# Two score chunks at a time, PSUM releases ranked first, and an output tile cut in three, in a fused attention and GELU kernel

## The chip, the cores and the metric

The kernel runs on one core of one Trainium2 chip. A core has five engines with instruction streams of their own: TensorE (matrix products, PE in the profile), VectorE (DVE), ScalarE (ACT), GpSimd (POOL) and SyncE (SP, which here only starts transfers). TensorE writes to PSUM, a small memory of eight banks, from which VectorE and ScalarE bring results back to the main on-chip memory. Transfers to and from device memory run on 16 DMA engines, fed by queues of SP, ScalarE and GpSimd.

The metric is the device time of one execution in microseconds (us), the median over several runs.

## What is computed

```python
# q, k, v: 8 batches x 12 heads x 448 x 64, float32
q_n = q / (norm(q) + 1e-06)
k_n = k / (norm(k) + 1e-06)
scores = q_n @ k_n.T / tau                  # tau = 0.1
attn = exp(scores - max); attn /= sum(attn)
x = (attn @ v)                              # heads side by side: 3584 x 768
h = x @ w_in                                # 768 x 2048
g = h * sigmoid(1.702 * h)
out = g @ w_out                             # 2048 x 768, float32
```

Each query's 448 scores lie within 1/tau of zero, so the kernel subtracts no maximum that depends on the data.

## The kernel before

**Work items.** Two heads of a batch make a pair `x`; there are 48, six to a batch. A pair is loaded (`load`), squared on ScalarE (`square`), summed and turned into inverse norms on VectorE, scaled to fp16 on GpSimd (`scale`; the queries of pair 0 on VectorE), and transposed, for pairs 0 to 11 on TensorE and VectorE, later by a DMA on SP's queue. From pair 12 on (batches 2 to 7) a pair's scores come in four chunks of 112 keys. One chunk (`scores`, L383 to L392) is two matmuls of 448 columns, one for each head, each using 64 of TensorE's 128 rows, into one `sp` tile of two PSUM banks; there are two such tiles. ScalarE takes the exponential of a chunk (`exp`, L397). Two attention products per pair follow (`attend`, L412: 16 matmuls into one bank `a`), each normalised by VectorE (`normalise`, L423 and L426, called `nx`), which frees the bank; then a DMA transposes the result (`turn`, L436). Pairs 0 to 11 do the same in halves of the queries (`scores_h`, `attend_h`, `normalise_h`, `turn_h`, `turned_h`), with the attention in one of the three `mm` banks, which the copy `turned_h` (called `x`) frees.

**The second part.** For each batch 16 products with `w_in` (`mm1`, L511: six matmuls of 448 columns) are followed by a tanh on ScalarE (`tanh`, L521) and a gate on VectorE (`gate`, L528), which frees the product's `mm` bank. The products with `w_out` (`mm2`, L566) run over output tiles of 128 tokens `t`, 28 in all, in two column halves `n` of `NW` = 384; a half is 16 matmuls, planned in four parts. ScalarE scales each half by 0.5 into `ost` (`halve`, L577), and `store` (L591 to L597) writes a tile in one or two runs of rows (`segments`). Only the last tile is stored half by half.

**What sets the order.** Nothing of the order is left to a scheduler in the compiler. `Plan` holds every operation with its engine, an assumed duration, a due time, what must precede it (`after`), and what buffers it takes and frees. `Plan.order` plays all engines forward in time: an engine that is idle starts, of its ready operations whose buffers are free, the one with the smallest due time. An operation on TensorE that changes between 64-row and 128-row matmuls is given `SWITCH_US` more. The order found is what each engine's stream is built in; at run time every engine works strictly through its stream. In the first 50 us of the plan, gaps on TensorE are filled with idle transposes (`fill`, L357).

Due times: a pair's scores, attention and `nx`/`x` are due at `s` to `s + 3`, with `s` two per pair (one per pair in batch 0); reductions 8 (4) before; the tail operations of products, that is tanh, gate and `ost`, `URGENT` = 12 before their product:

```python
add(("s", x, c), "PE", 0.19, s + c // 2, partial(scores, x, c), after=[("qkT", x)],
    takes=[("sp", 1)], frees=[("qkT", int(c == C - 1))], rows=64)
...
add(("nx", x, j), "DVE", 0.55, s + 2 + j, partial(normalise, x, j), after=[("at", x, j)],
    takes=[("xf", 1 - j)], frees=[("a", 1)])
```

Of the kernel before, what the change touches and what calls it, by code (L numbers as in the profile page):

```python
# [10 lines left out]
FP32 = mybir.dt.float32  # L11
# [7 lines left out]
RS_A, RS_B = 0.703952253, 0.703952253 * 2.38924456  # L19

SEM_US = 0.1
SWITCH_US = 0.12
DMA_US = 1.9
LATE_FROM, LATE_US, URGENT = 80.0, 2.0, 12
DMA_ENGINES, DMA_PKT_US, DMA_KB_US = 16, 0.024, 0.037
# [129 lines left out]
def kernel(  # L155
# [23 lines left out]
    AHEAD = 3  # L179
    SQP, SQT, XA, CA, TA, POW = (), (0, 1), (), (0, 1), (), range(HP, 2 * HP)  # L180
    TURN = 2 * HP
    SH = S // 2
    inv_tau = float(1.0 / tau)
    shift = max(0.0, inv_tau - 10.0)
# [195 lines left out]
    def queries(x, j, s0, s1):  # L380
        return qkTs[x][64 * j : 64 * (j + 1), 1, s0:s1]

    def scores(x, c):  # L383
        sp = sps[x, c] = ps_s.tile([128, 2, 512], FP32, name="sp")
        for j in range(2):
            nc.tensor.matmul(  # L386
                out=sp[:, j, :S],
                lhsT=keys(x, j, c),
                rhs=queries(x, j, 0, S),
                start=True,  # L390
                stop=True,
            )  # L392

    def exp(*key):
        e = exps[key] = ets[len(exps) % NE]
# [153 lines left out]
    def gate_h(h, m):  # L549
# [9 lines left out]
            op1=ALU.mult,  # L559
        )  # L560

    def mm2(b2, t, n, part):
        if part == 0:
            mms[b2, t, n] = ps_m.tile([128, 512], FP32, name="mm")
        for kk in range(4 * part, 4 * part + 4):
            nc.tensor.matmul(  # L566
                out=mms[b2, t, n][:, :NW],
                lhsT=gts[b2][:, kk, 128 * t : 128 * (t + 1)],
                rhs=w_out_sb[:, kk, NW * n : NW * (n + 1)],
                start=(kk == 0),  # L570
                stop=(kk == KT2 - 1),
            )

    def halve(b2, t, n):
        if n == 0:
            osts[b2, t] = p_o.tile([128, DM], FP32, name="ost")
        nc.scalar.activation(  # L577
            out=osts[b2, t][:, NW * n : NW * (n + 1)],
            in_=mms.pop((b2, t, n))[:, :NW],
            func=AF.Copy,  # L580
            scale=0.5,
        )
# [5 lines left out]
            yield i0, n  # L588
            i0 += n

    def store(b2, t, i0, n, cols):  # L591
        b, c, p0 = 2 * b2 + i0 // S, (i0 % S) // P, i0 % P
        rows = out[b * S : (b + 1) * S].rearrange("(p c) m -> c p m", c=C)[c]
        nc.sync.dma_start(
            out=rows[p0 : p0 + n, cols],
            in_=osts[b2, t][i0 - 128 * t : i0 - 128 * t + n, cols],
        )  # L597
# [31 lines left out]
    for x in range(NPAIR):  # L629
# [3 lines left out]
        for ti, nm in ((1, "k"), (0, "q")):  # L633
            add(("load", nm, x), "ACT" if x + ti == 0 else "SP", 0.5, s - 13, partial(load, x, (q32, k32)[ti], (q, k)[ti], nm + "32"),
                takes=[(nm, 1)], dma=PAIR, hold=hold, turn=True)
            pl = sq_pool(x, ti)
            add(("sq", ti, x), "POOL" if pl else "ACT", 1.0 if pl else 0.53, early + ti * 0.1, partial(square, x, ti),
                after=[("load", nm, x)], takes=[("sq", 1), ("port", int(pl))], frees=[("port", int(pl))])
            add(("red", ti, x), "DVE", 0.6, early + 0.2, partial(reduce, x, ti),
                after=[("sq", ti, x)], frees=[("sq", 1)])  # L640
            dve = x == 0 and ti == 0
            add(("scale", ti, x), "DVE" if dve else "POOL", 0.7 if dve else 1.0, early + 0.5 if first else s - 5 - ti * 0.1,
                partial(scale, x, ti, nc.vector if dve else nc.gpsimd),
                after=[("norm", 1, grp)], takes=[("qks", 1), ("port", 1)], frees=[(nm, 1), ("port", 1)])
# [25 lines left out]
        if x < HALF:  # L670
            for h in range(2):
                sh = x + HP * h if first else s + h
                for u in range(2):
                    key = (x, h, u)
                    add(("s",) + key, "PE", 0.2, sh, partial(scores_h, *key), after=[("qkT", x)] + [("s", min(x + AHEAD, HP - 1), 0, 1)] * (first and h),
                        takes=[("sp", 1)], frees=[("qkT", h * u)], rows=64)
                    add(("exp",) + key, "ACT", 0.82, sh + 0.1, partial(exp, *key), after=[("s",) + key],
                        takes=[("exp", 1)], frees=[("sp", 1)])
                es = [("exp", x, h, u) for u in range(2)] + [("cast", x)]
                add(("at", x, h), "PE", 0.48, sh + 1, partial(attend_h, x, h), after=es,  # L680
                    takes=[("mm", 1)], frees=[("exp", 2), ("vt", h)])
                add(("nx", x, h), "DVE", 0.65, sh + 1, partial(normalise_h, x, h), after=[("at", x, h)],
                    takes=[("xs", 1)])
                add(("turn", x, h), "PE", 0.15, sh + 1, partial(turn_h, x, h), after=[("nx", x, h)],
                    frees=[("xs", 1)])
                add(("x", x, h), "ACT" if x in XA and not h else "DVE", 0.35, sh + 1, partial(turned_h, x, h), after=[("turn", x, h)],
                    takes=[("x", 1 - h)], frees=[("mm", 1)])
            continue
        for c in range(C):
            add(("s", x, c), "PE", 0.19, s + c // 2, partial(scores, x, c), after=[("qkT", x)],  # L690
                takes=[("sp", 1)], frees=[("qkT", int(c == C - 1))], rows=64)
            add(("exp", x, c), "ACT", 0.82, s + c // 2 + 0.1, partial(exp, x, c),
                after=[("s", x, c)], takes=[("exp", 1)], frees=[("sp", 1)])
        for j in range(2):
            es = [("exp", x, c) for c in range(C)] + [("cast", x)]
            if j == 1:
                es.append(("nx", x, 0))
            add(("at", x, j), "PE", 0.475, s + 2 + j, partial(attend, x, j), after=es,
                takes=[("a", 1)], frees=[("exp", 4 * j), ("vt", j)])
            add(("nx", x, j), "DVE", 0.55, s + 2 + j, partial(normalise, x, j), after=[("at", x, j)],  # L700
                takes=[("xf", 1 - j)], frees=[("a", 1)])
        add(("x", x), "SP", 1.0, s + 4, partial(turn, x), after=[("nx", x, 1)],
            takes=[("x", 1)], frees=[("xf", 1)], dma=packets(256, 512))
# [11 lines left out]
    for b in range(B):  # L715
# [18 lines left out]
                  [("g", int(b % 2 == 0 and u == units[0]))], [("th", 1), ("mm", 1)])])  # L734
        tiles = (0, 1, 2) if b % 2 == 0 else (3, 4, 5, 6)
        for t in tiles:
            for n in range(2):
                for part in range(4):
                    if b:
                        after = [("g", b, 4 * part + 3)]  # L740
                    else:
                        after = [("g", h, 4 * part + 2, "h") for h in range(1 + (t > 0))]
                    after.append(("w_out", part // 2))
                    after += [("mm2", b2, t, n, part - 1)] if part else []
                    last = t == tiles[-1] and n == 1 and part == 3
                    tail = []
                    if part == 3:
                        tail = [("ost", "ACT", 0.4, partial(halve, b2, t, n), [("ost", 1 - n)], [("mm", 1)])]
                        split = b == B - 1 and t == tiles[-1]
                        if n == 1 or split:  # L750
                            cols = slice(NW * n, NW * (n + 1)) if split else slice(0, DM)
                            segs = list(segments(b2, t))
                            for i, (i0, rows) in enumerate(segs):
                                tail.append((("st", i), "SP", packets(rows, 4 * (cols.stop - cols.start)),
                                    partial(store, b2, t, i0, rows, cols), [],
                                    [("ost", int(n == 1 and i == len(segs) - 1))]))
                    product(("mm2", b2, t, n, part), 0.652, partial(mm2, b2, t, n, part), after,
                        [("mm", int(part == 0))], [("g", int(last and b % 2))], tail)

    total, done = sum(u[1] for u in moe), 0.0  # L760
    for name, us, emit, after, takes, frees, tail in moe:
        b, part = divmod(B * done / total, 1)
        start, end = moe_due(b), moe_due(b + 1)
        due = start + (end - start) * part
        done += us
        add(name, "PE", us, due, emit, after=after, takes=takes, frees=frees)
        prev = name
        for kind, eng, n, e, tk, fr in tail:
            if eng == "SP":
                add(kind + name[1:], eng, 0.5, due, e, after=[prev], frees=fr, dma=n)  # L770
            else:
                me = (kind,) + name[1:]
                before = [prev]
                if kind == "ost":
                    me = me[:-1]
                    if me[-1]:
                        before.append(me[:-1] + (0,))
                add(me, eng, n, due - URGENT, e, after=before, takes=tk, frees=fr)
                prev = me
    for i in range(2):  # L780
# [55 lines left out]
```

## Time and profile before

| | |
|---|---|
| median of 13 runs | 439.76 us (438.3 to 440.81) |
| the profiled execution's own time | 439.13 us |
| its span, first to last instruction | 437.3 us |
| TensorE busy | 424.9 us (97%), 4161 matmuls |
| VectorE busy | 237.4 us (54%) |
| ScalarE busy | 306.9 us (70%) |
| GpSimd busy | 151.3 us (35%) |
| granted TensorE clock | 0.998 of full speed |
| exponentials L397 | 192, mean 920 ns |
| products L511, L566 | 672 of 448 columns, 896 of 384 columns |

The span is what the profiler saw from the first to the last instruction; the execution's time is 1.8 us longer. In the tables below a line number such as L386 is that of the kernel before. Busy times of matmuls count each from its start to its modelled end, and since matmuls overlap, the cost of one is the distance to the start of the next.

### The profile page before, as it was taken

The numbers are of one execution on the slowest core, as the hardware profiler recorded it, in microseconds if no ns is written. First come the engines' busy times: TensorE is split into PE (matmuls) and PEld (weight loads), VectorE is DVE, ScalarE is ACT, GpSimd is POOL, SyncE is SP. The second block draws the span as 40 slices with busy tenths as digits, with TensorE's granted clock in tenths as the row PEclk, the third lists the DMA queues.
The fourth block names the chain that finished last, engine by engine and source line by source line (L and its number), as shares of the span: only waits on it lengthen the run. The fifth ranks groups of instructions, "written<-read, shape, count | busy, mean of one in ns | idle before, by whom it ended". The sixth has DMA issues, their size and how long they took to land.

```text
span 437.3 us, 10541 instructions
## 1 busy us (share of the span) xinstructions
PE 424.9 (97%) x4161; PEld 260.1 (59%) x4161; DVE 237.4 (54%) x612; ACT 306.9 (70%) x490; POOL 151.3 (35%) x203
## 2 busy tenths in 40 slices
PE   8899999999999998999999999999999999999996
PEld 8668777555555654565555655565555655565563
DVE  4767978885886759653775338641542125404400
ACT  5899977859999868767896678766776566314411
POOL 2843997375527564242060604242100000000000
PEclk9999999999999999999999999999999999999999
DMA  8999397999997999477555676565112130021022
GB/s 233 250 229 254 76 209 186 274 252 286 211 211 157 257 221 228 116 162 180 155 132 153 175 182 135 142 116 136 35 26 48 49 97 14 12 73 36 2 72 72
DMA packets 95888, 63.99 MB, mean 146 GB/s; under 512 B 56288, under 2 KB 90848, under 8 KB 95840
## 3 DMA queue, kind: packets, MB, share of 16 engines
q1 hardware_dynamic: 91952, 56.81, 55.3%
q0 software_dynamic: 3648, 6.29, 8.0%
q8 instruction: 32, 0.52, 0.5%
q10 hardware_dynamic: 240, 0.23, 0.2%
q14 instruction: 16, 0.13, 0.1%
HBM read 45.61 MB, written 11.01 MB: 129 GB/s over the span
## 4 chain that ended last, share of the span: by engine, by line
PE 60%; DMA 2%; POOL 1%; DVE 1%; SPq 0%; ACT 0%; issue 0%; DVEq 0%; ACTq 0%
PE mm L566 26%; PE mm L511 24%; PE avp L412 6%; PE sp L386 5%; POOL qks L325 1%; DMA k<-in_k_dram 1%; DMA qkT<-qks 1%; DVE gT L528 0%; DVE n L251 0%; SPq L232 0%; SPq L366 0%; ACT sq L245 0%; ACT ost L577 0%; DVE t L291 0%; DVE t L280 0%
## 5 line engine op out<-in xcount | busy, mean ns | idle before, releaser
L397 ACT ACTIVATE et<-sp 112x896 f16<-112x896 f32 x192 | 167.4, 920 | 37.2 <-PE sp L386 32.4
L566 PE MATMUL mm<-w_out,gT 128*128 128x384 f16 x896 | 154.7, 326 | 0.6 <-ACT ost L577 0.6
L511 PE MATMUL mm<-xT,w_in 128*128 128x448 f16 x672 | 135.4, 353 | 1.4 <-DVE gT L528 1.4
L566 PEld LDWEIGHTS <-gT 128*128 128x128 f16 x896 | 83.8, 98 | 66.0 <-issue 14.2
L511 PEld LDWEIGHTS <-w_in 128*128 128x128 f16 x672 | 62.4, 98 | 69.0 <-issue 15.6
L528 DVE SCALAR_TENSOR_TENSOR gT<-th,mm 128x448 f16<-128x448 f16 x112 | 68.7, 616 | 61.0 <-ACT th L521 61.0
L521 ACT ACTIVATE th<-mm 128x448 f16<-128x448 f32 x128 | 69.9, 549 | 33.4 <-PE mm L511 30.5
L251 DVE TENSOR_REDUCE n<-sq 112x8 f32<-112x512 f32 x96 | 63.2, 677 | 28.0 <-ACT sq L245 27.7
L341 POOL CAST vt<-v 112x256 f16<-112x256 f32 x92 | 35.0, 404 | 118.6 <-PE avp L412 70.9
L577 ACT ACTIVATE ost<-mm 128x384 f32<-128x384 f32 x56 | 27.7, 495 | 44.9 <-PE mm L566 43.3
L412 PEld LDWEIGHTS <-et 112*128 112x128 f16 x1152 | 44.6, 97 | 11.4 <-issue 0.2
L325 POOL TENSOR_TENSOR qks<-k,y 112x512 f16<-112x512 f32 x36 | 37.6, 1045 | 31.4 <-DVE y L292 23.2
L423 DVE RECIPROCAL rcx<-avp 128x4 f32<-128x4 f32 x72 | 12.9, 180 | 63.0 <-PE avp L412 62.4
L412 PE MATMUL avp<-vt,et 112*128 112x65 f16 x1152 | 46.7, 193 | 0.0
L386 PE MATMUL sp<-qkT 64*128 64x448 f16 x288 | 40.9, 355 | 0.0
L325 POOL TENSOR_TENSOR qks<-q,y 112x512 f16<-112x512 f32 x36 | 37.6, 1045 | 0.0
L245 ACT ACTIVATE sq<-k 112x512 f32<-112x512 f32 x48 | 30.4, 637 | 6.5 <-DMA k<-in_k_dram 5.2
L426 DVE TENSOR_TENSOR xf<-avp,rcx 128x256 f16<-128x256 f32 x72 | 30.5, 424 | 2.5
L245 ACT ACTIVATE sq<-q 112x512 f32<-112x512 f32 x48 | 30.4, 638 | 1.6 <-DVE n L251 1.4
L541 PE MATMUL mm<-xT,w_in 128*128 128x224 f16 x192 | 21.0, 259 | 0.9 <-DVE gT L553 0.9
L308 POOL TENSOR_TENSOR n<-n,root_of 112x16 f32<-112x16 f32 x6 | 17.4, 2904 | 11.7 <-DVE n L251 11.7
L357 PE MATMUL tps<-ident 128*128 128x128 f16 x241 | 18.1, 234 | 3.2 <-DVE qkT L361 1.8
(44 smaller groups left out, 229.6 us busy)
## 6 DMA issues: line engine op xcount, KB each, us to landing
k<-in_k_dram SPq DMA_DIRECT2D x48, 224.0 KB, 4.4
v<-in_v_dram SPq DMA_DIRECT2D x48, 224.0 KB, 4.8
q<-in_q_dram SPq DMA_DIRECT2D x47, 224.0 KB, 4.7
w_in<-in_moe_w_in_dram POOLq DMA_DIRECT2D x2, 1536.0 KB, 16.2
w_out<-in_moe_w_out_dram POOLq DMA_DIRECT2D x2, 1536.0 KB, 14.4
out_dram<-ost SPq DMA_DIRECT2D x7, 336.0 KB, 3.2
out_dram<-ost SPq DMA_DIRECT2D x8, 288.0 KB, 2.8
out_dram<-ost SPq DMA_DIRECT2D x8, 240.0 KB, 3.0
```

Source lines behind the costliest of these rows:

```text
L245: return nc.scalar.activation(out=sqs[x, ti], in_=src, func=AF.Square)
L251: nc.vector.tensor_reduce(out=n2s[grp][:, x - grp[0], ti], in_=sqs.pop((x, ti)), axis=AX.X, op=ALU.add,)
L325: return eng.tensor_tensor(out=qkss[x][:, 1 - ti].rearrange("p c j d -> p j c d"), in0=src, in1=rss[x][:, ti, :, :, None].to_broadcast((P, ...
L341: copy(out=vt[:, :, j, :D], in_=src[:, j]) for j in range(2)
L386: nc.tensor.matmul(out=sp[:, j, :S], lhsT=keys(x, j, c), rhs=queries(x, j, 0, S), start=True, stop=True,)
L397: nc.scalar.activation(out=e[:, : 2 * S].rearrange("p (j s) -> p j s", j=2), in_=sps.pop(key)[:P, :, :S], func=AF.Exp, scale=inv_tau, **kw,)
L412: nc.tensor.matmul(out=ps[:, (D + 1) * t : (D + 1) * (t + 1)], lhsT=exps[x, c][:, q0 : q0 + 128], rhs=values(x, c, D * j, D * j + D + 1), ...
L426: nc.vector.tensor_tensor(out=xfs[x][:, :, j], in0=ps[:, :, j : j + D], in1=r[:, :, None].to_broadcast((128, 4, D)), op=ALU.mult,)
L511: nc.tensor.matmul(out=ps[:, :S], lhsT=w_in_sb[:, kk, 128 * m : 128 * (m + 1)], rhs=xTs[b, kk][:, :S], start=(kk == 0), stop=(kk == KT1 - 1),)
L521: nc.scalar.activation(out=ths[key], in_=mms[key][:, :S], func=AF.Tanh, scale=0.851)
L528: nc.vector.scalar_tensor_tensor(out=gts[b // 2][:, m, (b % 2) * S : (b % 2 + 1) * S], in0=ths.pop((b, m)), scalar=1.0, in1=mms.pop((b, m) ...
L566: nc.tensor.matmul(out=mms[b2, t, n][:, :NW], lhsT=gts[b2][:, kk, 128 * t : 128 * (t + 1)], rhs=w_out_sb[:, kk, NW * n : NW * (n + 1)], st ...
```

## The change

1. The plan's entry for scores now stands for two chunks: `scores(x, c0)` issues chunks `c0` and `c0 + 1`, four matmuls, and takes both `sp` tiles at once. Each exponential still waits for the scores and frees its own tile. `SWITCH_US` goes from 0.12 to 0.1.
2. The due times of `nx` and `x` are lowered by `URGENT`, so they rank with gates.
3. The queries of pair 5 are scaled on VectorE too (`SD`).
4. The last output tile has three column parts, 384, 192 and 192, each with its own `halve` and stores. Of the last part's two stores, the first (16 rows) is started from ScalarE's queue, the second (112 rows) from SP's.

```diff
-SWITCH_US = 0.12
+SWITCH_US = 0.1
...
+    SD = ((0, 0), (5, 0))
...
-    def scores(x, c):
-        sp = sps[x, c] = ps_s.tile([128, 2, 512], FP32, name="sp")
-        for j in range(2):
+    def scores(x, c0):
+        for c in (c0, c0 + 1):
+            sp = sps[x, c] = ps_s.tile([128, 2, 512], FP32, name="sp")
+            for j in range(2):
...
+    def cuts(b2, t):
+        if (b2, t) == (B // 2 - 1, 2 * S // 128 - 1):
+            return (0, NW), (NW, NW + NW // 2), (NW + NW // 2, DM)
+        return (0, NW), (NW, DM)
+
     def mm2(b2, t, n, part):
+        c0, c1 = cuts(b2, t)[n]
...
-                out=mms[b2, t, n][:, :NW],
+                out=mms[b2, t, n][:, : c1 - c0],
                 lhsT=gts[b2][:, kk, 128 * t : 128 * (t + 1)],
-                rhs=w_out_sb[:, kk, NW * n : NW * (n + 1)],
+                rhs=w_out_sb[:, kk, c0:c1],
...
-            dve = x == 0 and ti == 0
+            dve = (x, ti) in SD
...
-                add(("nx", x, h), "DVE", 0.65, sh + 1, partial(normalise_h, x, h), after=[("at", x, h)],
+                add(("nx", x, h), "DVE", 0.65, sh + 1 - URGENT, partial(normalise_h, x, h), after=[("at", x, h)],
...
-                add(("x", x, h), "ACT" if x in XA and not h else "DVE", 0.35, sh + 1, partial(turned_h, x, h), after=[("turn", x, h)],
+                add(("x", x, h), "ACT" if x in XA and not h else "DVE", 0.35, sh + 1 - URGENT, partial(turned_h, x, h), after=[("turn", x, h)],
...
-            add(("s", x, c), "PE", 0.19, s + c // 2, partial(scores, x, c), after=[("qkT", x)],
-                takes=[("sp", 1)], frees=[("qkT", int(c == C - 1))], rows=64)
+            if c % 2 == 0:
+                add(("s", x, c), "PE", 0.38, s + c // 2, partial(scores, x, c), after=[("qkT", x)],
+                    takes=[("sp", 2)], frees=[("qkT", c // 2)], rows=64)
             add(("exp", x, c), "ACT", 0.82, s + c // 2 + 0.1, partial(exp, x, c),
-                after=[("s", x, c)], takes=[("exp", 1)], frees=[("sp", 1)])
+                after=[("s", x, c // 2 * 2)], takes=[("exp", 1)], frees=[("sp", 1)])
...
-            add(("nx", x, j), "DVE", 0.55, s + 2 + j, partial(normalise, x, j), after=[("at", x, j)],
+            add(("nx", x, j), "DVE", 0.55, s + 2 + j - URGENT, partial(normalise, x, j), after=[("at", x, j)],
...
-                        split = b == B - 1 and t == tiles[-1]
-                        if n == 1 or split:
-                            cols = slice(NW * n, NW * (n + 1)) if split else slice(0, DM)
+                        split = len(cuts(b2, t)) > 2
+                        if end or split:
+                            cols = slice(c0, c1) if split else slice(0, DM)
...
+                                alone = split and end and i == 0
+                                tail.append((("st", i), "ACT" if alone else "SP", packets(rows, 4 * (cols.stop - cols.start)),
+                                    partial(store, b2, t, i0, rows, cols, nc.scalar if alone else nc.sync), [],
```

Since the plan is played anew with these entries, the order of all engines' streams changes along the whole kernel, not only at these places.

More of the change, by code (lines that the diff above doesn't have):

```diff
@@ L381, in queries @@
         return qkTs[x][64 * j : 64 * (j + 1), 1, s0:s1]
-    def scores(x, c):
-        sp = sps[x, c] = ps_s.tile([128, 2, 512], FP32, name="sp")
-        for j in range(2):
[L386 to L392, printed above, removed]
+    def scores(x, c0):
+        for c in (c0, c0 + 1):
+            sp = sps[x, c] = ps_s.tile([128, 2, 512], FP32, name="sp")
+            for j in range(2):
+                nc.tensor.matmul(
+                    out=sp[:, j, :S],
+                    lhsT=keys(x, j, c),
+                    rhs=queries(x, j, 0, S),
+                    start=True,
+                    stop=True,
+                )
     def exp(*key):
@@ L576, in halve @@
             osts[b2, t] = p_o.tile([128, DM], FP32, name="ost")
+        c0, c1 = cuts(b2, t)[n]
         nc.scalar.activation(
-            out=osts[b2, t][:, NW * n : NW * (n + 1)],
-            in_=mms.pop((b2, t, n))[:, :NW],
+            out=osts[b2, t][:, c0:c1],
+            in_=mms.pop((b2, t, n))[:, : c1 - c0],
             func=AF.Copy,
@@ L589, in segments, with store @@
             i0 += n
-    def store(b2, t, i0, n, cols):
+    def store(b2, t, i0, n, cols, eng):
         b, c, p0 = 2 * b2 + i0 // S, (i0 % S) // P, i0 % P
         rows = out[b * S : (b + 1) * S].rearrange("(p c) m -> c p m", c=C)[c]
-        nc.sync.dma_start(
+        eng.dma_start(
             out=rows[p0 : p0 + n, cols],
@@ L736 @@
         for t in tiles:
-            for n in range(2):
+            for n, (c0, c1) in enumerate(cuts(b2, t)):
+                end = n == len(cuts(b2, t)) - 1
                 for part in range(4):
@@ L744 @@
                     after += [("mm2", b2, t, n, part - 1)] if part else []
-                    last = t == tiles[-1] and n == 1 and part == 3
+                    last = t == tiles[-1] and end and part == 3
                     tail = []
                     if part == 3:
-                        tail = [("ost", "ACT", 0.4, partial(halve, b2, t, n), [("ost", 1 - n)], [("mm", 1)])]
-                        split = b == B - 1 and t == tiles[-1]
-                        if n == 1 or split:
-                            cols = slice(NW * n, NW * (n + 1)) if split else slice(0, DM)
+                        tail = [("ost", "ACT", 0.4, partial(halve, b2, t, n), [("ost", int(n == 0))], [("mm", 1)])]
+                        split = len(cuts(b2, t)) > 2
+                        if end or split:
+                            cols = slice(c0, c1) if split else slice(0, DM)
                             segs = list(segments(b2, t))
                             for i, (i0, rows) in enumerate(segs):
[L754 to L757, printed above, removed]
+                                alone = split and end and i == 0
+                                tail.append((("st", i), "ACT" if alone else "SP", packets(rows, 4 * (cols.stop - cols.start)),
+                                    partial(store, b2, t, i0, rows, cols, nc.scalar if alone else nc.sync), [],
+                                    [("ost", int(end and i == len(segs) - 1))]))
+                    product(("mm2", b2, t, n, part), 0.652 * (c1 - c0) / NW, partial(mm2, b2, t, n, part), after,
                         [("mm", int(part == 0))], [("g", int(last and b % 2))], tail)
@@ L768 @@
         for kind, eng, n, e, tk, fr in tail:
-            if eng == "SP":
+            if kind[0] == "st":
                 add(kind + name[1:], eng, 0.5, due, e, after=[prev], frees=fr, dma=n)
@@ L776 @@
                     if me[-1]:
-                        before.append(me[:-1] + (0,))
+                        before.append(me[:-1] + (me[-1] - 1,))
                 add(me, eng, n, due - URGENT, e, after=before, takes=tk, frees=fr)
```

## The prediction

> **What bounds the kernel now.** I read the stage table first: busy time of each engine in stretches cut where the trace changes character. (Columns: stretch, its length, then busy us and instruction count of each engine, granted clock, DMA share, GB/s.)
>
> ```profile
> 11.00:33.00 22.00, 19.52 (x351) 15.21 (x350) 15.25 (x42) 18.94 (x33) 13.87 (x20) 1.00 1.12 239
> 33.00:51.00 18.00, 16.57 (x232) 14.25 (x228) 14.91 (x35) 17.37 (x29) 11.55 (x8) 1.00 0.85 191
> 51.00:95.00 44.00, 42.82 (x540) 30.46 (x537) 36.36 (x97) 33.68 (x52) 32.09 (x37) 1.00 1.02 216
> 95.00:140.00 45.00, 45.00 (x456) 24.25 (x455) 32.48 (x83) 44.12 (x69) 25.84 (x39) 1.00 0.95 219
> 140.00:158.00 18.00, 18.00 (x180) 10.84 (x178) 13.64 (x42) 15.31 (x27) 9.98 (x12) 1.00 1.12 234
> 158.00:172.00 14.00, 12.58 (x96) 6.58 (x95) 8.92 (x25) 9.93 (x17) 6.52 (x10) 1.00 0.90 218
> 172.00:370.00 198.00, 198.00 (x1812) 113.47 (x1811) 94.51 (x242) 141.64 (x219) 48.74 (x73) 1.00 0.50 117
> 370.00:433.00 63.00, 62.90 (x378) 35.64 (x376) 15.87 (x28) 18.96 (x38) 0.00 (x0) 1.00 0.16 43
> ```
>
> The first number after the length is TensorE. From 95 us on it has no gap, except 1.42 us in 158 to 172. Before 95 it lacks 5.1 us from 11 on. Its clock is full. So the end is set by how much work its stream holds, by those gaps, and by what follows its last matmul at 432.90. ScalarE is as full (44.12 of 45) in one stretch, 95 to 140.
>
> Next, the timeline of TensorE there (start, duration, line). Matmuls overlap, so cost is start to next start.
>
> ```profile
> 97.80 1.31 PE L511 MATMUL mm<-xT,w_in 128*128 128x448 f16 x6
> 99.04 0.36 PE L386 MATMUL sp<-qkT 64*128 64x448 f16 x2
> 99.34 1.31 PE L511 MATMUL mm<-xT,w_in 128*128 128x448 f16 x6
> ...
> 101.17 1.31 PE L511 MATMUL mm<-xT,w_in 128*128 128x448 f16 x6
> 102.32 0.65 PE L412 MATMUL avp<-vt,et 112*128 112x65 f16 x16
> 102.90 0.55 PE L386 MATMUL sp<-qkT 64*128 64x448 f16 x4
> 103.38 1.31 PE L511 MATMUL mm<-xT,w_in 128*128 128x448 f16 x6
> ```
>
> Six 448-wide matmuls take 1.15 us ahead of attention (101.17 to 102.32) but 1.24 ahead of a score chunk: 0.09 to enter the 64-row form. One chunk occupies 0.30 (99.04 to 99.34), two together 0.48, so a chunk is 0.18 to 0.19 and leaving the form costs 0.11. **A visit to the 64-row form costs 0.20 us beside its work.**
>
> Then the end, and the one gap behind 95 us.
>
> ```profile
> 432.94 0.49 ACT L577 ACTIVATE ost<-mm 128x384 f32<-128x384 f32 x1 [2.06 <-PE mm L566]
> 433.45 0.78 SPq L594 DMA_DIRECT2D out_dram<-ost  x2
> ...
> out_dram<-ost SPq DMA_DIRECT2D x1, 168.0 KB, 2.2
> out_dram<-ost SPq DMA_DIRECT2D x1, 24.0 KB, 1.5
> ```
>
> ```profile
> 163.19 0.63 ACT L245 ACTIVATE sq<-k 112x512 f32<-112x512 f32 x1 [2.17 <-DMA k<-in_k_dram]
> 163.85 0.69 DVE L251 TENSOR_REDUCE n<-sq 112x8 f32<-112x512 f32 x1 [2.18 <-ACT sq L245]
> ...
> PE mm L511 <- DVE gT L528: 1.4, 3, 0.8
> ```
>
> After the last matmul come 0.49 us of evacuation, two stores issued one after the other (0.39 each), and a landing of 2.2. In the gap a late k load held ScalarE's square, behind it the tanh, and on VectorE the gates; products then waited 1.4 us in three places for their PSUM bank.
>
> **The change, part by part.** I counted the changed kernel's instruction order, which is fixed when the kernel is built.
>
> *Score pairs.* Before, 144 chunks of batches 2 to 7 stand in 78 visits: 66 pairs and 12 singles, all singles between 99 and 139 us. After, 72 visits. That removes 6 x 0.20 = 1.2 us where TensorE has no gap. Replanning also packs the scores of batches 0 and 1 (L448) into 34 visits, not 37: 3 x 0.20 = 0.6. Their price is the same (a lone visit 0.30, a double 0.49), but they lie ahead of 95 us, where gaps may swallow it; I take half, bounds 0 and 0.6. Together **1.5 us**.
>
> *What pairing waits for.* A pair needs both `sp` buffers. In the plan it is issued when both exponentials before it are done, so TensorE does products meanwhile. In the trace a pair starts at 157.51, its two exponentials run from 157.91 to 159.64: 2.13 us after the pair started. Here a rule of the Trainium skill speaks against the change: "TensorEngine Tiling (Array Packing)", section PSUM Bottleneck, says that row tiling speeds up TensorE but not the emptying of PSUM. By the rule, ScalarE paces 95 to 140: it has 2% to spare there, and each pair leaves it some 0.4 us (157.51 to 157.91) without input if nothing else is queued. The 34 chunks there (11 visits of two, 12 of one) make 17 pairs, 6.8 us, and if that reached the end the sum below would turn from -2.6 into 4.2. By the rows it reaches the attention's lead only: counted by start-to-start durations, between the last attention of batch 2 and the first product that needs it stand 25.8 us of TensorE work before, 12.6 after. The result needs about 0.6 (normalising) + 1.2 (transpose issue) + 2.5 (landing), 4.3 in all, and at the longest landing seen (5.4) 7.2. The lead halves and still covers. For batches 4 to 7 the leads are unchanged (32.8, 29.9, 32.8, 21.8). I follow the rows: 0 us by this way.
>
> *Two tighter places.* From batch 2's scores to the start of batch 4's, attention now follows its own last pair by 1.96 us of work in four places (least elsewhere 2.27, as before, but for two places, 1.33 and 1.70, where the last chunk was a single and one exponential was left). Exponentials end 2.13 after the pair's start; attention's slot is at 0.48 + 1.96 = 2.44: 0.3 in hand. A tanh in front (0.55) would overdraw it. And second attentions follow first ones by 1.24 us in nine places, where VectorE's normalising (0.18 + 0.42, 0.83 from slot end to its last result, as 145.74 to 146.57 in the timeline) leaves 0.4; a reduce in front (0.68) would overdraw it. Before, two stood at 1.05 and TensorE waited in neither. Bounds: 0, and 13 x 0.35 = 4.6. I take **0.6 lost**, near the row without a wait.
>
> *VectorE's releases first.* `nx` and `x` now rank ahead of reductions; no instruction is added. Their gain is inside the order already counted. Queued behind a release are gates and reductions: a gate comes at most 0.6 us later. Three products' worth of PSUM (`mm=3`, 1.15 us each) covers that; without cover it is the 0.2 to 0.8 per product of the gap shown. The gap itself rests on SP's queue (transposes waiting for GpSimd's scaling, then v, k, q behind them). After, the loads stand at least 6.5 us of TensorE work ahead of their squares around there, against 5.9 and 5.6 before; a load takes 4.4 to land. I take half of 1.4: **0.7 gained**, bounds -1.0 and 1.4. The queries of pair 5 are scaled on VectorE (0.69, the one such row) and not on GpSimd (1.04), at about 25 us, where filler transposes keep TensorE busy: nothing. Fillers are 240, not 241: 0.07.
>
> *Last tile.* The last 384 columns become 192 + 192. Matmuls: 16 x 0.163 (the final 128 take 20.81) against 32 at what a 192-wide one costs. From the 224-wide row (1.16 for 12, 0.097 each) and the 384-wide one the slope is 0.41 ns per column, so 0.084: 2.69 against 2.60, **0.08 lost**. A second rule speaks against it: the same page, section Instruction Overhead, gives every matmul some 60 cycles; at the 2.4 columns per ns of the 448-wide row (0.189 each) 16 more would be 0.4 us. The rows hold 3 ns beyond the streaming, so I take 0.08. Evacuation: ScalarE's rows give (920 - 549) / 448 = 0.83 ns per column; 192 fewer are **0.16**. The 112-row store no longer queues behind the 16-row one, which goes to ScalarE's queue: **0.39**. Landing of 84 KB by the two rows: 1.5 + 60/144 x 0.7 = 1.8: **0.4**, bounds 0 and 0.5. The middle part's two stores are issued (0.78) within the 1.34 us of the last part's matmuls. Together **0.9 gained**; 0.4 at worst.
>
> Sum: -1.5 + 0.6 - 0.7 - 0.1 - 0.9 = **-2.6 us**. The profiled execution took 439.13, of which 437.3 is span: it becomes 436.5. It stood 0.63 below the median of 439.76, so in the median I forecast **437.2**.
>
> **Rivals.** (0.2%, about 0.9 us, is the least that this measurement tells from no change.)
>
> *The saved visits are swallowed:* TensorE's work shrinks but small waits grow by as much in 95 to 160, and only the end's part stays, with a landing that saves 0.2 and not 0.4. For it: ScalarE at 98%. Against: before, singles stood there for no visible wait. 439.76 - 0.7 = 439.1.
>
> *The tight places decide:* each of the 13 costs a third of a microsecond because VectorE or ScalarE is mid-instruction when its input comes, 4.6 us, and the lead is too short to be given back. 439.76 - 1.5 - 0.9 - 0.1 + 4.6 = 441.9. From 0.19 us each it eats the gain of 2.5, from 0.26 the kernel is measurably slower. For it: slack 0.3 against instructions of 0.55 and 0.68. Against: 1.05 passed without a wait.
>
> That pairs are not made is excluded by the order: 72 of 72.
>
> **How the numbers follow.** Forecast 0.68, swallowed 0.17, tight places 0.15. The forecast's own range is 435.6 to 438.9 (bounds of the early visits, the gap, the tail and up to 1.8 of waits). Faster: 0.66 of the first, 0.06 of the second, 0.72. Same: 0.02 + 0.10 + 0.01 = 0.13. Slower: 0.15. The range 435.3 to 440.1 leaves out the third and a fringe of the first.
>
> **What would show it.** TensorE's score rows in 95 to 140 all x4; its last matmul 1.3 to 2.0 us earlier; ScalarE with idle time before L397's counterpart while TensorE stays at 45 of 45; the last store issued about 0.35 us behind TensorE's last matmul, the span ending some 3.5 behind it where it was 4.4. Wrong, if TensorE shows waits for exponentials or normalising between 105 and 160 summing above 1.5 us, or a new gap of gates as at 165, or more gaps ahead of 95.

## The result and the profile after

The changed kernel takes 436.53 us (median of 11 runs, 435.1 to 437.53) against 440.1 (48 runs of the kernel before): ratio 0.9916, 95% interval 0.9898 to 0.9933, that is 3.0 to 4.5 us less. Forecast were 2.6 us less and 437.2. The profiled execution took 435.8 us with a span of 433.8, against 439.13 and 437.3.

The stage table of the changed kernel, same columns as before:

```profile
11.00:33.00 22.00, 19.06 (x343) 14.66 (x340) 15.86 (x42) 18.19 (x33) 12.94 (x19) 1.00 1.12 236
33.00:51.00 18.00, 16.71 (x242) 15.23 (x243) 13.51 (x35) 16.25 (x26) 10.09 (x7) 1.00 0.82 202
51.00:95.00 44.00, 43.07 (x543) 30.89 (x541) 35.55 (x91) 35.57 (x54) 31.60 (x36) 1.00 0.93 210
95.00:140.00 45.00, 43.99 (x414) 23.72 (x412) 33.80 (x91) 39.14 (x64) 28.31 (x39) 1.00 1.02 214
140.00:158.00 18.00, 18.00 (x184) 10.01 (x181) 10.03 (x30) 16.52 (x27) 6.27 (x11) 1.00 1.06 263
158.00:172.00 14.00, 14.00 (x138) 7.38 (x136) 10.94 (x24) 12.76 (x21) 7.55 (x11) 1.00 0.95 191
172.00:370.00 198.00, 198.00 (x1840) 112.98 (x1837) 97.45 (x255) 145.27 (x222) 51.12 (x75) 1.00 0.52 119
```

The gap in 158 to 172 is gone (12.58 became 14.00). A new one of 1.01 us stands in 95 to 140. ScalarE's busy time in that stretch went from 44.12 to 39.14. That is mainly another order and not lost time: 25 exponentials run there, where 34 did. Two of the 25 waited for their scores, 2.1 us in all, where none had waited, and TensorE waited for no exponential:

```profile
126.80 0.92 ACT L399 ACTIVATE et<-sp 112x896 f16<-112x896 f32 x1 [0.92 <-PE sp L388]
...
138.91 0.92 ACT L399 ACTIVATE et<-sp 112x896 f16<-112x896 f32 x1 [1.22 <-PE sp L388]
```

The new gap, in the changed kernel's timeline:

```profile
94.29 1.30 PE L513 MATMUL mm<-xT,w_in 128*128 128x448 f16 x6
95.62 0.54 ACT L523 ACTIVATE th<-mm 128x448 f16<-128x448 f32 x1 [1.19 <-PE mm L513]
96.06 0.87 ACT L587 ACTIVATE ost<-mm 128x384 f32<-128x384 f32 x2
96.60 3.56 PE L513 MATMUL mm<-xT,w_in 128*128 128x448 f16 x18 [1.01 <-ACT ost L587]
```

ScalarE's stream has the tanh of the first product ahead of two evacuations whose products are done. The tanh must wait for the product; the next product waits for a bank that the evacuation behind the tanh frees.

The end, from the timelines and the transfer table:

```profile
430.33 0.33 ACT L587 ACTIVATE ost<-mm 128x192 f32<-128x192 f32 x1 [0.99 <-PE mm L575]
430.70 0.35 ACTq L604 DMA_DIRECT2D out_dram<-ost  x1
...
430.90 0.38 SPq L604 DMA_DIRECT2D out_dram<-ost  x1
...
out_dram<-ost SPq DMA_DIRECT2D x2, 84.0 KB, 1.8
```

The last matmul ends at 430.30, the span 3.54 us later, where it was 4.35.

**Where 3.4 us of span came from** (437.25 and 433.84 before rounding). Executions differ by up to 1.3 us in when the first pair's data are there, whatever the kernel. A mark behind that start, the first filler that waits for VectorE (11.63 us before, 12.01 after), takes this out. From the mark to the last matmul TensorE needs 2.99 us less:

| | us |
|---|---|
| nine visits to the 64-row form fewer, at 0.215 (measured below) | -1.94 |
| the gap of gates: three starts late by 0.38, 0.50, 0.96 (start to start) | -1.84 |
| the new gap: 94.29 to 96.60 where a product takes 1.135 | +1.18 |
| ten gaps of over 0.15 us behind the mark and ahead of 95 us became eight: idle 4.05 and 3.98, and by estimate 0.17 for each | -0.4 |
| last tile's 16 more matmuls | +0.04 |
| one filler fewer | -0.07 |
| sum | -3.03 |

With 0.81 at the end, less 0.38 of later start, the 2.99 make 3.4. The table is an account of one execution of each kernel and not exact: with gaps down to 0.06 us counted too, its fourth row is -0.2 and the sum -2.8. The largest of the three late starts, before (2.09 us from start to start, where a product takes 1.135):

```profile
167.81 1.29 PE L511 MATMUL mm<-xT,w_in 128*128 128x448 f16 x6 [0.43 <-DVE gT L528]
169.90 2.43 PE L511 MATMUL mm<-xT,w_in 128*128 128x448 f16 x12 [0.79 <-DVE gT L528]
```

### The profile page after: what moved, and what is told of

The parts are those of the page before. It is cut to its first block, busy times and chain, and to the rows that moved or that the text cites. A ratio compares the mean times of both kernels' runs of the same rounds, so it can differ in the third digit from the quotient of the medians.

```text
span 433.8 us, 10578 instructions
## 1 busy us (share of the span) xinstructions
PE 422.8 (97%) x4176; PEld 259.6 (60%) x4176; DVE 236.7 (55%) x613; ACT 308.7 (71%) x491; POOL 150.5 (35%) x202
## 4 chain that ended last, share of the span: by engine, by line
PE 89%; DVE 4%; POOL 3%; ACT 2%; issue 2%; POOLq 0%; ACTq 0%
PE mm L575 34%; PE mm L513 30%; PE avp L414 8%; PE sp L388 8%; PE tps L358 4%; PE mm L467 2%; PE sp L450 1%; POOL n L309 1%; PE mm L543 1%; ACT et L399 1%; POOL qks L326 1%; DVE gT L555 1%; DVE n L252 1%; PE tps L350 1%; DVE qkT L362 1%
## 5 line engine op out<-in xcount | busy, mean ns | idle before, releaser
L575 PE MATMUL mm<-w_out,gT 128*128 128x384 f16 (+1 forms) x912 | 156.3, 324 | 0.4 <-ACT ost L587 0.4
L587 ACT ACTIVATE ost<-mm 128x384 f32<-128x384 f32 (+1 forms) x57 | 27.6, 487 | 42.8 <-PE mm L575 41.2
L388 PE MATMUL sp<-qkT 64*128 64x448 f16 x288 | 39.7, 354 | 0.0
```

What stands on the lines that cost most here:

```text
L388: nc.tensor.matmul(out=sp[:, j, :S], lhsT=keys(x, j, c), rhs=queries(x, j, 0, S), start=True, stop=True,)
L575: nc.tensor.matmul(out=mms[b2, t, n][:, : c1 - c0], lhsT=gts[b2][:, kk, 128 * t : 128 * (t + 1)], rhs=w_out_sb[:, kk, c0:c1], start=(kk == 0),
```

## The experiments

Each kernel is timed against runs of the kernel before on its own chip; ratios are to those. Line numbers of an experiment are its own.

**1. The last tile alone.** Everything of the change undone but the cut of the last tile and the second queue.

```diff
-SWITCH_US = 0.1
+SWITCH_US = 0.12
...
+    def scores(x, c):
...
-                add(("nx", x, h), "DVE", 0.65, sh + 1 - URGENT, partial(normalise_h, x, h), after=[("at", x, h)],
+                add(("nx", x, h), "DVE", 0.65, sh + 1, partial(normalise_h, x, h), after=[("at", x, h)],
```

> The kernel before with the last output tile alone cut in three and its last 16-row store on ScalarE's queue; everything ahead of that tile is in the old order. The forecast's sum: last matmul where it was (+0.08 us), last evacuation 0.33 and not 0.49, 112-row store issued 0.37 behind the last matmul and not 0.94, span 0.9 us shorter behind the matmuls. If the saved landing is not real (rival 'swallowed'), 0.4 to 0.7.

Ratio 0.9976 (0.9959 to 0.9993), 1.1 us. The last 112-row store was issued 0.39 us behind the last matmul and the span ended 3.53 behind it, 0.82 less than before: about as forecast.

```profile
433.25 0.32 SPq L602 DMA_DIRECT2D out_dram<-ost  x1
433.25 0.38 ACTq L602 DMA_DIRECT2D out_dram<-ost  x1
...
out_dram<-ost ACTq DMA_DIRECT2D x1, 12.0 KB, 1.9
```

The gap of gates was there, with 0.68 us and not 1.42: its size differs between executions of one order.

**2. Pairs alone.** The kernel before with `scores(x, c0)` and its plan entry.

> The kernel before with scores of batches 2 to 7 two by two, nothing else. Visits of the 64-row form: 72 + 37 where they were 78 + 37. If a visit costs 0.20 us wherever it stands: TensorE's work 1.2 us less. If the gap of gates at 165 us was a matter of the old order of loads, it goes too: 2.6 us less in all; if it comes from something else, 1.2 only. If tight places decide: waits for exponentials or normalising between 105 and 160, up to 4.6 us slower.

Ratio 0.9936 (0.9912 to 0.9961), 2.8 us, beside the 2.6 of the first theory. The profile has no gap of gates. The one execution profiled was 0.7 us faster only, because of a wait at 82 us:

```profile
79.81 0.63 ACT L245 ACTIVATE sq<-k 112x512 f32<-112x512 f32 x1 [1.45 <-DMA k<-in_k_dram]
...
82.18 0.37 PE L449 MATMUL sp<-qkT 64*128 64x224 f16 x4 [1.60 <-ACT et L398]
```

A k load came late; the square that needs it held up the exponentials behind it in ScalarE's stream. It lies ahead of the pairs, in batch 1.

**3. Releases first alone.**

```diff
-                add(("nx", x, h), "DVE", 0.65, sh + 1, partial(normalise_h, x, h), after=[("at", x, h)],
+                add(("nx", x, h), "DVE", 0.65, sh + 1 - URGENT, partial(normalise_h, x, h), after=[("at", x, h)],
```

(and the same for the other two entries.)

> The kernel before with normalising and xT copies ranked 12 us earlier, nothing else. Visits 79 + 36, fillers 237. The forecast: adds no instruction and gains nothing by itself, so within 0.5 us of before. A theory in which early release is what shortens the kernel: 1 us or more faster, by smaller gaps ahead of 95 us.

Ratio 0.9989 (0.9972 to 1.0007): no difference that can be told. The gap of gates stayed (2.4 us).

**4. The change without the tail.** The last tile has two halves, as in the kernel before.

> The changed kernel with the last tile in two halves as before. If the tail's 0.9 us is additive to the rest: 0.9 us slower than the changed kernel, i.e. 2.6 us faster than before; last matmul 0.08 earlier than in the changed kernel.

Ratio 0.9935 (0.9912 to 0.9958), 2.9 us faster than before. From the mark, the last matmul came 0.06 us earlier than in the changed kernel, and the span ended 4.36 behind it, not 3.54. In the traces the tail adds to the rest; the two ratios' intervals overlap.

**5. Pairs pulled apart, same order.** In batches 4 to 7 the second chunk of a pair is issued behind the next piece of TensorE's stream that is no score.

```diff
+        chunk(c0)
+        if x >= 4 * HP:
+            plan.late = partial(chunk, c0 + 1)
+        else:
+            chunk(c0 + 1)
```

> The changed kernel in the same order, but in batches 4 to 7 the second chunk of each of the 48 pairs is issued one piece of TensorE's stream later. No work is added, 48 visits to the 64-row form are. At 0.20 us a visit: 9.6 us slower, all of it between 200 and 370 us. If the cost of a visit is hidden elsewhere (the rival in which saved visits are swallowed): less than 3 us.

446.5 us, ratio 1.0167 (1.013 to 1.0204). From the first score of batch 2 to the start of the last attention TensorE took 279.6 us, 269.27 in the changed kernel, without a new wait between: 10.33 / 48 = 0.215 us a visit. In its timeline:

```profile
251.66 0.36 PE L392 MATMUL sp<-qkT 64*128 64x448 f16 x2
251.95 0.82 PE L585 MATMUL mm<-w_out,gT 128*128 128x384 f16 x4
252.71 0.36 PE L392 MATMUL sp<-qkT 64*128 64x448 f16 x2
253.00 2.77 PE L585 MATMUL mm<-w_out,gT 128*128 128x384 f16 x16
```

Four matmuls of 384 columns, 0.652 otherwise, take 0.76 ahead of the second chunk, and each chunk 0.29. A visit's price is real and is not hidden anywhere where TensorE has no gap.

**6. The second queue undone.**

```diff
-                                alone = split and end and i == 0
+                                alone = False
```

> The changed kernel with the last 16-row store on SP's queue like the others. By the sum: the 112-row store is issued 0.39 us later and the span is 0.4 us longer. If the second queue does nothing: no difference.

435.76 us, ratio 0.9917 (0.989 to 0.9945): no difference that can be told. In the profile the 112-row store was issued 0.39 us behind the last evacuation, as computed, and the span ended 3.71 behind the last matmul, 0.17 later than with the second queue. In the changed kernel that store went out 0.23 behind its evacuation, not 0.03: SP was not free. It issued the first part's 112-row store at 428.63 for 1.24 us (0.41 before the change), and the middle part's two after that, until 430.80. Over the nine profiled kernels with that cut this issue took from 0.41 (run 10) to 1.24 us (the changed one and run 5); why is open. It did not set the end: in runs 1, 8, 9, 10 and 12 SP was free, the last store went out 0.03 us behind its evacuation, and the span ended 3.48 to 3.54 behind the last matmul, against 3.54 in the changed kernel.

**7. Three output tiles.**

```diff
-    p_o = pool("p_o", 2)
+    p_o = pool("p_o", 3)
...
-        | dict(x=2 * HP, mm=3, th=3, g=1, ost=2, port=1)
+        | dict(x=2 * HP, mm=3, th=3, g=1, ost=3, port=1)
```

> The changed kernel with three output tiles in place of two. In the changed kernel one product near 96 us waits 1.0 us for a PSUM bank that an evacuation frees, which stands behind a tanh in ScalarE's stream. If it was placed there because the plan saw no free output tile: that gap closes and the kernel is 1.0 us faster. If the plan's place has another cause: no difference.

434.76 us, ratio 0.9889 (0.9868 to 0.9909). The gap at 96 us is gone, and from the mark the last matmul came 1.07 us earlier than in the changed kernel. The plan had put the evacuations behind the tanh because it saw no free output tile. That the kernel gains rests on the trace, since the intervals of the two ratios overlap.

**8. The change without pairs.** `scores` and its plan entry as before, all else changed.

> The changed kernel with scores issued one by one. Visits 80 + 34 in place of 72 + 34: 8 x 0.20 = 1.6 us slower by visits alone. If the gap of gates was tied to singles and their hurry, it comes back with 1 us or more on top; if releases first removed it, it does not.

Ratio 0.9969 (0.9955 to 0.9984); 438.83 us, 2.3 more than the changed kernel, of which eight visits at 0.215 are 1.7. The profiled execution is one of the two slowest of 22 (440.56), its span 4.9 more. In it the gap of gates is back:

```profile
166.60 0.63 ACT L246 ACTIVATE sq<-k 112x512 f32<-112x512 f32 x1 [2.19 <-DMA k<-in_k_dram]
...
168.53 1.29 PE L512 MATMUL mm<-xT,w_in 128*128 128x448 f16 x6 [1.10 <-DVE gT L529]
```

All four profiled kernels with singles (before, 1, 3, 8) have this gap near 168 us, and none of those with pairs. It belongs to the order that singles lead to, not to the ranking. How large it is in other executions is not shown; the median leaves some 0.6 us for it and all other waits.

**9. The tight places made tighter.**

```diff
+        tight = j == 0 and x - HALF in (3, 4, 5, 6, 7, 11, 12, 13, 14)
+        for _ in range(3 if tight else 1):
             nc.vector.tensor_tensor(
```

> The changed kernel with the first normalising of nine pairs (those whose second attention follows the first by 1.24 us) done three times over, in the same order of all engines: some 0.78 us more between an attention and its freed bank in these nine places, nothing else. In the changed kernel's trace the second attention starts 0.27, 0.40, 0.40, 0.40, 0.41, 0.17, 0.40, 0.41 and 0.84 us after the release. If that slack is all there is and nothing is given back: eight waits that sum to 3.4 us, and 0.17 us more for each since the array runs empty (as beside the gaps of gates): 3.4 to 4.8 us slower. If the attention's lead absorbs such waits: less than 1 us.

441.76 us, ratio 1.0024 (1.0009 to 1.0039), 5.2 us more than the changed kernel by the medians.

```profile
132.69 0.65 PE L414 MATMUL avp<-vt,et 112*128 112x65 f16 x16
135.09 0.64 PE L414 MATMUL avp<-vt,et 112*128 112x65 f16 x16 [0.50 <-DVE xf L430]
```

Start to start is 2.40 where it was 1.72: 0.68 lost beside 0.50 of idle time, and so in most of the eight places that waited (the others more); from the mark to the last matmul 6.06 us more, of which some 5.7 are these waits. Nothing is given back by the attention's lead. The normalising's last record came about 0.92 us later behind the first attention, and of that 0.25 was free.

**10. The change without the ranking.**

> The changed kernel with normalising and xT copies at their old due times. Visits 72 + 39 in place of 72 + 34, fillers 247 in place of 240. At 0.215 us a visit and 0.07 a filler: 1.6 us slower. If ranking releases first has no use: no difference.

439.66 us, ratio 0.9983 (0.9963 to 1.0003): 3.1 more than the changed kernel by the medians, where visits and fillers explain 1.6. The 20 executions form two groups. In 13 the granted clock was 0.998 or more, and their median is 438.96, 2.4 more than the changed kernel; in 7 it was 0.996, and they took 440.88 to 442.43. The profiled one is the slowest of all. It has a late load at 155 us, and behind it 3.4 us at half the clock:

```profile
154.29 0.63 ACT L246 ACTIVATE sq<-k 112x512 f32<-112x512 f32 x1 [3.14 <-DMA k<-in_k_dram]
...
155.78 0.37 PE L388 MATMUL sp<-qkT 64*128 64x448 f16 x2 [1.66 <-ACT et L399]
...
157.20:160.60 3.40, 3.40 (x12) 1.49 (x10) 2.86 (x11) 2.22 (x4) 0.00 (x0) 0.50 1.14 285
```

The 12 products' matmuls from 157.85 on take 3.64 us there, where 12 take 2.27 elsewhere. (The clock is the third number from the end, 0.50.) Whether the wait brought the low clock is not shown; waits of 1.60 us (run 2) and 1.75 (run 3) came without one. What remains of the 2.4 beside the 1.6 was not taken apart; TensorE's waits behind the mark and ahead of 95 us sum to 5.8 us in that trace, 4.3 in the changed kernel.

**11. Three output tiles and a shorter end.** Parts of 384, 256 and 128 columns, all 16-row stores on ScalarE's queue.

```diff
-            return (0, NW), (NW, NW + NW // 2), (NW + NW // 2, DM)
+            return (0, NW), (NW, DM - 128), (DM - 128, DM)
...
-                                alone = split and end and i == 0
+                                alone = split and i == 0
```

> Three output tiles, the last tile cut into 384, 256 and 128 columns, and all three of its 16-row stores on ScalarE's queue. Against the kernel with three output tiles alone: last evacuation 0.28 and not 0.33, SP free when it ends so that the last store is issued 0.1 us sooner, landing of 56 KB a little sooner, matmuls 0.05 more: 0.1 to 0.4 us faster than that one, some 1.3 us faster than the changed kernel. If the middle part's evacuation is held up by the queue's issues on ScalarE: no gain or a loss.

434.54 us, ratio 0.9864 (0.9834 to 0.9895): 2.0 us under the changed kernel by the medians, and not told apart from 7 (434.76). SP was free: the last store went out 0.02 us behind its evacuation. From its issue to the end of the span it still took 2.96 us for 56 KB, where 84 KB took 2.94 in the changed kernel. The span ended 3.30 behind the last matmul (3.49 in 7), but that matmul came 0.35 later from the mark, 0.29 of it in a longer wait at 39 us.

**12. The two small edits undone** (`SD` with pair 0 alone, `SWITCH_US` 0.12).

> The changed kernel with the two small edits undone: the queries of pair 5 scaled on GpSimd again and SWITCH_US at 0.12. Visits 72 + 36 (not 72 + 34), fillers 237 (not 240). By visits and fillers alone: 0.43 - 0.21 = 0.2 us slower, no difference that can be measured. If each replanning shifts the waits ahead of 95 us and around 155 by as much as the kernels so far show (the kernel without ranking lost 3 us with 1.6 explained): anything up to 2 us slower, with new waits in these two places.

436.3 us, ratio 0.9929 (0.9915 to 0.9942), against 0.9916 (0.9898 to 0.9933) for the changed kernel: not told apart. In the profile there were new waits of 0.97 us at 51 and 0.76 at 142, one at 38 was longer (1.18 for 0.61), and the one at 96 was gone, though with two output tiles: that gap too belongs to a particular order.

## Why the forecast held, and where its terms were off

The gain by the medians was 3.6 us where 2.6 was forecast. Most of the difference lies ahead of the end: the last matmul was to come 1.3 to 2.0 us earlier and came 2.99 earlier from the mark (2.60 as the traces stand). Visits brought 0.4 more than charged, the tight places 0.6, the early gaps some 0.2 to 0.4; the last tile brought 0.1 less.

**Score pairs.** Right. The price read from two rows (0.20) was 0.215 when 48 visits were added (run 5), and all nine visits came off. That refutes the rival in which saved visits are swallowed.

**What pairing waits for.** Right. ScalarE waited 2.1 us for scores in 95 to 140, and TensorE waited for no exponential. The lead of batch 2's attention fell from 25.3 to 12.1 us, as counted, and covered it. The Trainium skill's rule that tiling speeds up TensorE but not the emptying of PSUM ("TensorEngine Tiling (Array Packing)", section PSUM Bottleneck) did not set the time here: ScalarE was busy for 39.14 of 45 us, since nine exponentials fewer run in that stretch, and products filled TensorE's time. "TensorE stays at 45 of 45" did not hold (43.99), by the gap at 96 us.

**Two tighter places.** I charged 0.6, it was 0; the slack ahead of the first attentions was read about rightly. In the changed kernel's timeline:

```profile
129.91 2.12 PE L575 MATMUL mm<-w_out,gT 128*128 128x384 f16 x12
129.97 1.72 ACT L399 ACTIVATE et<-sp 112x896 f16<-112x896 f32 x2
...
131.87 0.65 PE L414 MATMUL avp<-vt,et 112*128 112x65 f16 x16
```

The exponentials end at 131.69, attention starts at 131.87: 0.18 us to spare, in the other three places 0.24 to 0.32. Between the normalising's last result and the second attention lie 0.17 to 0.40 us in eight of the nine places, and 0.84 in the ninth, which is not tight. Of the slack that the prediction put at 0.4, 0.25 could be used (run 9). No tanh or reduce in front overdrew the slack; that the plan, which placed those too, saw to it is argued, not shown. The rival's mechanism is real, as run 9 shows at 0.66 us a place and more; its trigger was not there.

**The gap of gates.** "I take half of 1.4: 0.7 gained": it went whole, and was worth 1.84 in the profiled execution where 1.42 of idle time were shown: matmul records overlap, and from start to start each gap cost 0.07 to 0.18 more than its idle time. Runs 2, 3 and 8 tie it to singles. Against it stands the gap at 96 us, which the forecast did not see: 1.18, which three output tiles close (run 7). The net, 0.66, came close to 0.7 by two errors that cancel, which is luck.

**Releases first.** "No instruction is added. Their gain is inside the order already counted" holds for run 3. But with pairs the order without it is 2.4 to 3.1 us slower (run 10). I had counted visits and fillers of the whole change, so the sum contained it; as a statement on this edit alone it says too little. Pairs alone (2.8), tail alone (1.1) and ranking alone (0.5, not sure) add up to 4.4, the whole is 3.6; with intervals of about 1 us on each side, that these differ is not shown.

**Last tile.** 0.77, close to the 0.9 of the forecast, but by terms that were off both ways. Evacuation took 0.33, as computed. Matmuls cost 0.04 (computed 0.08): they follow each other at 82.5 ns, and the 0.4 reckoned from the Trainium skill ("TensorEngine Tiling (Array Packing)", section Instruction Overhead) did not show. From the last store's issue to the end of the span it took 3.44 us for 168 KB and 2.94 for 84: 0.50 saved, not 0.4 (to the landing alone 2.16 and 1.78). The second queue brought 0.17, not 0.39. "The middle part's two stores are issued (0.78) within the 1.34 us of the last part's matmuls" failed in the changed kernel, but where it held (runs 1, 8, 9, 10, 12) the end came no sooner. So the step that failed is that an earlier issue of the 112-row store brings the end forward by as much. In run 1 both last stores went out together and ScalarE's, of 12 KB, landed last, 1.9 us later; why it is no faster is open.

## What to carry to other kernels

Where an engine has no gaps, count what its stream holds, a mode change too: two rows of a trace gave its price within a tenth, and counting the new order gave the number of visits. A wait of TensorE costs more than the idle time shown, here by 0.07 to 0.18 us, so read it from start to start. An earlier issue of a last store is not an earlier end: look at what lands last. When a planner sets the order, an edit's worth is that of the whole new order: look for instructions that stand in a strict queue ahead of ready ones, such as an evacuation behind a tanh or exponentials behind the square of a late load.

## What the runs showed that was not expected

- Whatever the kernel, the start (first filler that waits for VectorE) lay between 11.2 and 12.5 us in the 14 profiled executions. That is more than several of the effects studied, so traces are best compared from that mark.
- A smaller last store stopped helping: 84 KB to 56 KB brought nothing (2.94 and 2.96 us from issue to the end of the span), 168 KB to 84 KB 0.50.
- Between a result's last record on VectorE and the start of the attention that waits for it lay 0.15 us in all eight waits of run 9, so 0.40 us of apparent slack held only 0.25.
- In 7 of 20 executions of run 10 the mean granted clock was 0.996, and in the one profiled that was 3.4 us at 0.50.
